# Re-ordered instructions and loads of batches 0 and 1, and a last quarter block split in three, in a linear-attention and gated-MLP kernel

## Chip, cores, metric

One core of a Trainium2 chip. The metric is device time in microseconds of one execution, median of several. A program on one core gives single runs that agree within about 0.35%.

## The reference

```python
q_s = exp(q - max(q, -1)); q_s /= sum(q_s, -1)          # batch 8, heads 8, seq 576, dim 64
k_s = exp(k - max(k,  2)); k_s /= sum(k_s,  2)
kv  = einsum('bhsd,bhse->bhde', k_s, v)
x   = einsum('bhsd,bhde->bhse', q_s, kv)                # to (4608, 512)
h   = x @ w_in                                          # 512 -> 2048
g   = h * sigmoid(beta * h)
out = g @ w_out                                         # 2048 -> 512
```

## The kernel before

Rows are worked in nine chunks: 512 positions of each batch, and the 64-row tails of all eight together. For each chunk TensorE makes x (4 tiles), then h in 16 slices j, each from 4 matmuls over kt; ScalarE makes the tanh, VectorE g, and TensorE adds g times w_out into accumulators ("acc"). The first two batches have their own code, written out instruction by instruction: each engine runs its own list in the order in which it is written. Heads go in pairs: `tpe` transposes the normalised q of a pair, `kvz_mm` makes its kv in 64x64 tiles of the array, `xpe` its x. Banks of PSUM are named by hand.

```python
def kvz_mm(b, j, tag=None, n=1):            # n pairs share one PSUM tile
    ...
    for i in range(RW):                     # 9
        for e in range(2):                  # the two heads: two 64x64 tiles of the array
            r = slice(e * D, (e + 1) * D)
            nc.tensor.matmul(t[r, 0, :], ek[b][r, j, ds(i * D, D)], va[b][r, j, i, :], ...,
                             tile_position=(e * D, e * D))

def kvz_norm(b, j, n=1):                    # VectorE: reciprocal, two multiplies into kvp
    ...
def warm(n, tag):                           # dummy 128x512 matmuls
    ...
# --- cut: the front, batch 0 (excerpt around h of w_in block 1) ---
    hpe(0, 4, [0], "b3")                    # j 4, kt 0, PSUM bank b3
    ...
    hpe(0, 5, [0], "b1")
    hpe(0, 5, [1])
    w_castk(1, 2, A)                        # ScalarE casts w_in block 1, kt 2
    ...
    hpe(0, 7, [0], "b2")
    ...
    hpe(0, 7, [1])
    hpe(0, 4, [2])                          # the first that needs that cast
    ...
    mm_b(0, 0)                              # the first acc matmuls
# --- cut: the end, last chunk; the fourth row block of 128 is two halves of 256 columns ---
    for st in range(1, R + 1):
        for j in range(HOLD + (st == 1), NJ):   # HOLD = 8: earlier j were done in the loop
            mm_b(LASTC, j, [st])
        store(LASTC, st)
```

The softmax here doesn't subtract the row's maximum and nothing guards it: scores larger than these inputs give would overflow.

## Time and profile before

| | before |
|---|---|
| median of the first 3 runs | 282.67 us (281.89 to 282.89) |
| span of the profiled run | 280.6 us |
| TensorE busy | 275.9 us, 98% |
| VectorE, ScalarE, GpSimd busy | 62%, 58%, 14% |
| first acc matmul of chunk 0 / of chunk 1 | 22.23 us / 50.22 us |
| start of the last copy, to the end of the span | 277.49, 3.11 us |

The kernel is a stream of TensorE matmuls with hardly a hole, so the useful marks are the starts of certain matmuls in the TensorE timeline: the first transposes (the dummies are over), the first acc of chunk 0 (the front is over), the first acc of chunk 1 (batch 1 is prepared), the last copy. Their differences tell where time goes to within about 0.05 us, which run times do not: these scatter by 1 us.

### The profile page before, as it was taken

How to read it: one execution, taken by the hardware profiler on the slowest of the kernel's cores; microseconds unless marked ns; L12 is line 12 of the kernel's file. 1: busy time of each engine (PE TensorE's matmuls, PEld its weight loads, DVE VectorE, ACT ScalarE, POOL GpSimd, SP SyncE). 2: the span in 40 equal slices, each digit the busy share in tenths (PEclk: the TensorE clock that was granted, in tenths of full speed). 3: DMA queues.
4: the chain of work that ended last, by engine and by line, in shares of the span. 5: the costliest groups of instructions: out<-in, count | busy, mean ns of one | idle time of the engine just before them, and what ended most of it. 6: DMA issues, size and time to landing. Idle time of an engine off the chain costs nothing.

```text
span 280.6 us, 4450 instructions
## 1 busy us (share of the span) xinstructions
PE 275.9 (98%) x1728; PEld 128.6 (46%) x1728; DVE 175.1 (62%) x284; ACT 162.8 (58%) x248; POOL 38.7 (14%) x58
## 2 busy tenths in 40 slices
PE   8999999999999999999999999999999999999995
PEld 2544454444444444444444444444444544445543
DVE  3864796994478446945595549553864596354361
ACT  4667985958486447744684559444733574454451
POOL 1554236133030003000300030000000000000000
PEclk9999999999999999999999999999999999999999
DMA  7999999999981993199418951641154034005003
GB/s 249 390 394 391 387 388 311 321 292 213 269 240 46 238 287 90 75 233 265 141 78 191 280 167 75 132 94 79 71 89 139 1 151 75 0 0 152 0 0 150
DMA packets 55172, 50.09 MB, mean 179 GB/s; under 512 B 26600, under 2 KB 47344, under 8 KB 55152
## 3 DMA queue, kind: packets, MB, share of 16 engines
q1 hardware_dynamic: 54224, 48.91, 59.8%
q10 hardware_dynamic: 928, 0.92, 0.9%
q8 instruction: 13, 0.21, 0.3%
q14 instruction: 7, 0.06, 0.1%
HBM read 36.71 MB, written 9.44 MB: 164 GB/s over the span
## 4 chain that ended last, share of the span: by engine, by line
PE 98%; DVE 1%; ACT 0%; issue 0%
PE h L403 44%; PE acc L452 43%; PE warm L531 3%; PE kv L341 2%; PE x L372 1%; PE acc L444 1%; PE kv L316 1%; PE x L388 1%; PE tp L297 1%; DVE eq L267 0%; DVE qsT L173 0%; ACT o L171 0%; DVE xT L612 0%; PE x L363 0%; PE tb L564 0%
## 5 line engine op out<-in xcount | busy, mean ns | idle before, releaser
L417 DVE SCALAR_TENSOR_TENSOR g<-th,h 128x512 bf16<-128x512 bf16 x144 | 96.2, 681 | 80.1 <-ACT th L413 79.8
L413 ACT ACTIVATE th<-h,beta_t 128x512 bf16<-128x512 f32 x144 | 97.9, 687 | 81.9 <-PE h L403 81.0
L403 PE MATMUL h<-xT,w_in_b 128*128 128x512 bf16 x576 | 143.2, 379 | 0.0
L452 PE MATMUL acc<-w_out_b,g 128*128 128x512 bf16 x560 | 141.0, 379 | 0.0
L403 PEld LDWEIGHTS <-w_in_b 128*128 128x128 bf16 x576 | 56.3, 98 | 66.4 <-ACT w_in_b L171 0.6
L452 PEld LDWEIGHTS <-g 128*128 128x128 bf16 x560 | 53.8, 98 | 66.0 <-issue 2.5
L173 POOL CAST va<-v_st 128x2048 bf16<-128x2048 f32 (+2 forms) x14 | 17.4, 1257 | 115.2 <-DMA v_st<-in_v_dram 115.2
L261 DVE TENSOR_REDUCE rq<-eq 128x16 f32<-128x1024 bf16 (+1 forms) x20 | 22.1, 1104 | 5.6 <-ACT eq L250 5.1
L267 DVE TENSOR_TENSOR eq<-eq,rq 128x1024 bf16<-128x1024 bf16 (+1 forms) x20 | 23.1, 1157 | 0.1
L171 ACT CAST xT<-x 128x512 bf16<-128x512 f32 x18 | 9.9, 588 | 17.8 <-PE x L372 14.9
L250 ACT ACTIVATE eq<-q_st 128x1024 bf16<-128x1024 f32 (+1 forms) x18 | 16.9, 955 | 2.9 <-DMA q_st<-in_q_dram 2.9
L173 DVE COPY o<-acc 128x512 f32<-128x512 f32 (+1 forms) x19 | 12.3, 660 | 3.6 <-PE acc L452 3.4
L171 ACT COPY o<-acc 128x512 f32<-128x512 f32 (+1 forms) x18 | 9.6, 577 | 8.4 <-PE acc L452 5.0
L173 DVE CAST xT<-x 128x512 bf16<-128x512 f32 x18 | 11.5, 684 | 2.5 <-PE x L372 1.8
L192 ACT ACTIVATE ek<-k_st 128x1024 bf16<-128x1024 f32 x12 | 12.6, 1051 | 0.0
L531 PE MATMUL warm<-xT 128*128 128x512 bf16 x30 | 10.0, 493 | 1.2 <-DVE xT L612 1.2
L173 POOL CAST w_in_b<-w_in 128x512 bf16<-128x512 f32 (+1 forms) x9 | 5.9, 663 | 4.9 <-DMA w_in<-in_moe_w_in_dram 4.7
L531 PEld LDWEIGHTS <-xT 128*128 128x128 bf16 x30 | 3.5, 122 | 6.1 <-issue 3.8
L173 POOL CAST w_out_b<-w_out 128x1024 bf16<-128x1024 f32 x5 | 5.2, 1041 | 7.4 <-DMA w_out<-in_moe_w_out_dram 7.4
L262 DVE RECIPROCAL rq<-rq 128x16 f32<-128x16 f32 (+1 forms) x20 | 4.9, 243 | 0.7
L341 PEld LDWEIGHTS <-ek 128*64 128x64 bf16 x192 | 4.1, 111 | 2.5 <-issue 2.5
L185 ACT ACTIVATE ek<-k_st 128x576 bf16<-128x576 f32 x8 | 5.1, 677 | 0.2 <-DMA k_st<-in_k_dram 0.2
(48 smaller groups left out, 83.1 us busy)
## 6 DMA issues: line engine op xcount, KB each, us to landing
out_dram<-o SPq DMA_DIRECT2D x14, 512.0 KB, 3.4
q_st<-in_q_dram SPq DMA_DIRECT2D x25, 256.0 KB, 4.2
k_st<-in_k_dram SPq DMA_DIRECT2D x6, 1024.0 KB, 9.2
v_st<-in_v_dram SPq DMA_DIRECT2D x6, 1024.0 KB, 11.3
w_in<-in_moe_w_in_dram SPq DMA_DIRECT2D x6, 512.0 KB, 9.6
v_st<-in_v_dram SPq DMA_DIRECT2D x8, 288.0 KB, 8.3
w_out<-in_moe_w_out_dram SPq DMA_DIRECT2D x4, 512.0 KB, 9.0
w_out<-in_moe_w_out_dram SPq DMA_DIRECT2D x2, 1024.0 KB, 9.3
```

Of the source, the lines that this page charges most:

```text
L171: eng.copy(dst, src)
L173: eng.tensor_copy(dst, src)
L192: nc.scalar.activation(ek[b][:, :, h, :].rearrange("p i h d -> p h i d"), k_st[b][:, h, 0 : R * D].rearrange("p h (i d) -> p h i d", i=R), ...
L250: nc.scalar.activation(eq[b][:, :, s * m : (s + 1) * m, :].rearrange("p i h d -> p h i d"), q_st[b][:, s * m : (s + 1) * m, :].rearrange(" ...
L261: nc.vector.tensor_reduce(rq[b][:, 0, :, h], eq[b][:, :, h, :], axis=AX.X, op=ALU.add)
L267: eng.tensor_tensor(eq[b][:, :, h, :], eq[b][:, :, h, :], rq[b][:, 1, :, h].unsqueeze(3).to_broadcast((P, R, m, D)), ALU.mult,)
L341: nc.tensor.matmul(t[r * D : (r + 1) * D, j, :], ek[b][:, i, hd, :] if i < R else ekt[(b // 2) % 2][:, ds(hd * D, D)], va[b][:, i, hd, :] ...
L403: nc.tensor.matmul(h[:], w_unit(j, kt), x_of(c)[:, kt, :], start=(kt == 0), stop=(kt == KT - 1),)
L413: nc.scalar.activation(th[:], h_of[c, j][:], ACTF.Tanh, scale=beta_t[:, j : j + 1])
L417: nc.vector.scalar_tensor_tensor(out=g[:], in0=th_of.pop((c, j))[:], scalar=1.0, in1=h_of[c, j][:], op0=ALU.add, op1=ALU.mult)
L452: nc.tensor.matmul(acc[st][:], g[:, ds(st * P, P)], w_out_b[:, j, :], start=(j == 0), stop=(j == NJ - 1),)
L531: nc.tensor.matmul(t[:], xT[2][:, 0, 0:P], xT[2][:, 0, :])
```

## The change

Its intent: give each engine an order fitted to landings of loads measured before, visit the 64x64 mode less often (batch 0: pairs 0 and 1 together; batch 1: pairs 0, 1, 2 in one run), and end with a shorter last piece. One dummy matmul less. The loads of batch 1 and w_out are re-ordered to match. Core of the diff:

```diff
+    ENDS = ((0, DM // 2), (DM // 2, DM // 4), (3 * DM // 4, DM // 4))
...
-    HB, AB = ["b1", "b2"], ["b0", "b3"]
+    HB, AB = ["b2", "b1"], ["b0", "b3"]
...                                        # store of the last chunk
+                last = st == R - 2 + len(ENDS)
+                evac(nc.scalar if last else nc.vector, o[:, R - 1, cols], acc[st][:, 0:hw])
...                                        # loads: beta before v of pair 1; k of batch 1 ahead of w_out
+    load_kv(k_st, k, 1, "k_st", [0])
     w_load("out", 1)
+    w_load("out", 2)
     load_q(1, 2, [0])
...                                        # front
-    warm(10, tag="acc2")
+    warm(8, tag="acc2")
...
+    warm(2, tag="acc0")
+    kvz_mm(0, 0, "acc3", 2)
     kz_exp(0, 2)
+    kvz_mm(0, 1)
...
+    hpe(0, 4, [0], "acc0")
...
     hpe(0, 5, [0], "b1")
     hpe(0, 5, [1])
...
+    th_act(0, 1)
+    hpe(0, 5, [2])                        # j 7 comes only later
...                                        # batch 1
+    kvz_mm(1, 0, "b0", 2)
+    kvz_mm(1, 1)
+    kvz_mm(1, 2, "b1", 1)
...
+    kvz_norm(1, 0, 2)
+    tpe(1, 3, "b2")
+    tpe(1, 2, "b3")
...
+    q_ev(1, 3, V)
+    xpe(1, 0, "b0")
+    q_ev(1, 2, V)
+    xpe(1, 1, "b2")
...
+    kvz_mm(1, 3, "b3", 1)
...                                        # the end
-    for st in range(1, R + 1):
-        for j in range(HOLD + (st == 1), NJ):
+    for st in range(1, R + 2):
+        if st > R:                         # the last 128 columns: all 16 j at the end
+            acc_of[LASTC].append(ps.tile([P, DM], F32, tag=bank("h"), ...))
+        for j in range(HOLD + (st == 1) if st <= R else 0, NJ):
             mm_b(LASTC, j, [st])
         store(LASTC, st)
```

More of the change, by code (lines that the diff above doesn't have):

```diff
@@ L442, in mm_b @@
             if c == LASTC and st >= R - 1:
-                hw = DM // 2
+                lo, hw = ENDS[st - R + 1]
                 nc.tensor.matmul(
@@ L446, in mm_b @@
                     g[:, ds((R - 1) * P, P)],
-                    w_out_b[:, j, ds((st - R + 1) * hw, hw)],
+                    w_out_b[:, j, ds(lo, hw)],
                     start=(j == 0),
@@ L507, in store @@
             if st >= R - 1:
-                hw = DM // 2
-                k_ = st - R + 1
-                cols = ds(k_ * hw, hw)
-                evac((nc.vector, nc.scalar)[k_], o[:, R - 1, cols], acc[st][:, 0:hw])
-                (nc.sync, nc.scalar)[k_].dma_start(ov[:, R - 1, cols], o[:, R - 1, cols])
+                lo, hw = ENDS[st - R + 1]
+                cols = ds(lo, hw)
+                last = st == R - 2 + len(ENDS)
+                evac(nc.scalar if last else nc.vector, o[:, R - 1, cols], acc[st][:, 0:hw])
+                (nc.scalar if last else nc.sync).dma_start(ov[:, R - 1, cols], o[:, R - 1, cols])
                 return
@@ L577 @@
     load_kv(v_st, v, 0, "v_st", [0])
+    nc.sync.dma_start(beta_r[:], moe_beta.rearrange("(hh q) -> hh q", q=2 * P))
     load_kv(v_st, v, 0, "v_st", [1])
     load_kv(v_st, v, 0, "v_st", [2])
-    nc.sync.dma_start(beta_r[:], moe_beta.rearrange("(hh q) -> hh q", q=2 * P))
     load_kv(v_st, v, 0, "v_st", [3])
@@ L589 @@
     w_load("out", 0, 1)
+    w_load("in", 2, 1)
     w_load("in", 2, 0)
-    w_load("in", 2, 1)
+    w_load("in", 3, 0)
     w_load("in", 3, 1)
-    w_load("in", 3, 0)
+    load_kv(k_st, k, 1, "k_st", [0])
     w_load("out", 1)
+    w_load("out", 2)
     load_q(1, 2, [0])
-    w_load("out", 2)
+    load_kv(k_st, k, 1, "k_st", [1])
     load_q(1, 2, [1])
+    w_load("out", 3, 0)
+    load_kv(k_st, k, 1, "k_st", [2])
+    load_kv(v_st, v, 1, "v_st", [1])
+    load_kv(v_st, v, 1, "v_st", [0])
     load_kv(v_st, v, 1, "v_st", [2])
-    w_load("out", 3, 0)
-    load_kv(k_st, k, 1, "k_st", [0])
-    load_kv(v_st, v, 1, "v_st", [0])
-    load_kv(k_st, k, 1, "k_st", [2])
-    load_kv(k_st, k, 1, "k_st", [1])
-    load_kv(v_st, v, 1, "v_st", [1])
-    w_load("out", 3, 1)
     load_kv(k_st, k, 1, "k_st", [3])
     load_kv(v_st, v, 1, "v_st", [3])
+    w_load("out", 3, 1)
     load_q(2)
@@ L621 @@
     q_sum(0, 0, 4)
-    q_exp(0, 3, 4)
     q_mul(0, 0, 4)
     q_exp(0, 2, 4)
-    q_sum(0, 3, 4)
-    tpe(0, 0, "acc3")
     q_exp(0, 1, 4)
     q_sum(0, 2, 4)
+    tpe(0, 0, "acc3")
+    q_exp(0, 3, 4)
+    q_sum(0, 1, 4)
     q_ev(0, 0, A)
-    q_sum(0, 1, 4)
     q_mul(0, 2, 4)
+    q_mul(0, 1, 4)
+    warm(8, tag="acc2")
+    tpe(0, 2, "acc3")
     kz_exp(0, 0)
-    q_mul(0, 1, 4)
-    warm(10, tag="acc2")
-    tpe(0, 2, "acc3")
-    kz_exp(0, 1)
     q_ev(0, 2, V)
-    vz_cast(0, 0, G)
     warm(1, tag="acc1")
@@ L640 @@
     tpe(0, 1, "acc2")
+    kz_exp(0, 1)
+    vz_cast(0, 0, G, part=0)
+    q_sum(0, 3, 4)
+    beta_pe("acc1")
+    vz_cast(0, 0, A, part=1)
+    vz_cast(0, 1, G, part=0)
+    vz_cast(0, 1, A, part=1)
     q_mul(0, 3, 4)
+    warm(2, tag="acc0")
+    kvz_mm(0, 0, "acc3", 2)
     kz_exp(0, 2)
-    warm(1, tag="acc1")
-    kvz_mm(0, 0, "acc3", 1)
-    vz_cast(0, 1, G)
-    q_ev(0, 1, V)
-    tpe(0, 3, "acc1")
-    kz_exp(0, 3)
-    kvz_norm(0, 0)
-    kvz_mm(0, 1, "acc2", 1)
-    vz_cast(0, 2, G)
@@ L652 @@
-    q_ev(0, 3, A)
-    beta_pe("acc0")
-    kvz_norm(0, 1)
-    kvz_mm(0, 2, "acc3", 1)
-    vz_cast(0, 3, A, part=1)
-    vz_cast(0, 3, G, part=0)
-    beta_ev()
-    xpe(0, 0, "acc1")
+    kvz_mm(0, 1)
+    vz_cast(0, 2, G, part=0)
+    tpe(0, 3, "acc0")
+    vz_cast(0, 2, A, part=1)
+    kvz_norm(0, 0, 2)
+    q_ev(0, 1, A)
+    kvz_mm(0, 2, "b3", 1)
+    vz_cast(0, 3, G)
+    kz_exp(0, 3)
+    xpe(0, 0, "b2")
     kvz_norm(0, 2)
-    kvz_mm(0, 3, "acc2", 1)
+    xpe(0, 1, "acc3")
     w_castk(0, 0, G)
@@ L663 @@
     xev(0, 0, A)
-    xpe(0, 1, "acc0")
-    kvz_norm(0, 3)
-    xpe(0, 2, "b3")
-    xev(0, 1, A)
-    hpe(0, 0, [0], "b0")
-    hpe(0, 1, [0], "b1")
-    xev(0, 2, V)
-    w_castk(0, 1, A)
+    kvz_mm(0, 3, "acc2", 1)
+    xev(0, 1, V)
+    q_ev(0, 3, A)
+    xpe(0, 2, "b3")
+    w_castk(0, 1, G)
+    hpe(0, 1, [0], "b0")
+    kvz_norm(0, 3)
+    hpe(0, 0, [0], "b1")
+    beta_ev()
+    xev(0, 2, A)
+    hpe(0, 3, [0], "b2")
+    hpe(0, 1, [1])
+    w_castk(0, 2, A)
     xpe(0, 3, "acc3")
-    w_castk(0, 2, G)
@@ L674 @@
-    hpe(0, 3, [0], "b2")
+    hpe(0, 3, [1])
+    w_castk(0, 3, G)
     xev(0, 3, V)
-    hpe(0, 2, [0], "acc0")
     hpe(0, 0, [1])
-    w_castk(0, 3, G)
-    hpe(0, 3, [1])
+    hpe(0, 2, [0], "b3")
     hpe(0, 3, [2])
-    hpe(0, 1, [1])
-    hpe(0, 1, [2])
-    hpe(0, 1, [3])
-    hpe(0, 3, [3])
-    th_act(0, 1)
-    w_castk(1, 0, G)
+    hpe(0, 2, [1])
     hpe(0, 0, [2])
     hpe(0, 0, [3])
-    hpe(0, 2, [1])
-    w_castk(1, 1, G)
-    th_act(0, 3)
-    hpe(0, 2, [2])
-    g_dve(0, 1)
-    hpe(0, 2, [3])
@@ L695 @@
-    hpe(0, 4, [0], "b3")
-    th_act(0, 0)
+    w_castk(1, 0, G)
+    hpe(0, 2, [2])
+    th_act(0, 0)
+    hpe(0, 2, [3])
+    hpe(0, 3, [3])
+    w_castk(1, 1, G)
+    hpe(0, 4, [0], "acc0")
+    th_act(0, 2)
+    hpe(0, 1, [2])
+    g_dve(0, 0)
+    hpe(0, 1, [3])
+    w_castk(1, 3, G)
     hpe(0, 4, [1])
-    g_dve(0, 3)
-    w_castk(1, 3, G)
+    w_castk(1, 2, A)
+    g_dve(0, 2)
     hpe(0, 5, [0], "b1")
     hpe(0, 5, [1])
-    w_castk(1, 2, A)
-    g_dve(0, 0)
-    hpe(0, 7, [0], "b2")
@@ L705 @@
-    th_act(0, 2)
-    hpe(0, 7, [1])
-    hpe(0, 4, [2])
-    hpe(0, 5, [2])
-    hpe(0, 4, [3])
-    g_dve(0, 2)
-    hpe(0, 5, [3])
-    th_act(0, 4)
+    th_act(0, 1)
+    hpe(0, 5, [2])
+    hpe(0, 4, [2])
+    th_act(0, 3)
+    hpe(0, 4, [3])
+    g_dve(0, 1)
+    hpe(0, 5, [3])
+    hpe(0, 7, [0], "b3")
+    th_act(0, 4)
+    hpe(0, 7, [1])
+    g_dve(0, 3)
     hpe(0, 7, [2])
+    w_cast("out", 0, 0, G)
     hpe(0, 7, [3])
+    th_act(0, 5)
+    g_dve(0, 4)
     hpe(0, 6, [0], "b0")
-    w_cast("out", 0, 0, G)
@@ L717 @@
-    th_act(0, 5)
     hpe(0, 6, [1])
-    g_dve(0, 4)
+    th_act(0, 7)
     hpe(0, 6, [2])
+    g_dve(0, 5)
     hpe(0, 6, [3])
-    th_act(0, 7)
-    g_dve(0, 5)
     mm_b(0, 0)
-    th_act(0, 6)
-    w_cast("out", 0, 1, G)
+    w_cast("out", 0, 1, A)
     g_dve(0, 7)
     mm_b(0, 1)
+    th_act(0, 6)
+    w_castk(2, 2, A)
+    mm_b(0, 2)
     g_dve(0, 6)
+    w_castk(2, 3, A)
+    mm_b(0, 3)
     w_castk(2, 0, A)
     w_castk(2, 1, G)
-    mm_b(0, 2)
-    mm_b(0, 3)
-    w_castk(2, 2, A)
-    w_castk(2, 3, G)
@@ L736 @@
-    hpe(0, 11, [0, 1, 2, 3], "b0")
-    w_cast("in", 3, 1, A)
-    hpe(0, 10, [0, 1, 2, 3], "b1")
+    hpe(0, 8, [0, 1, 2, 3], "b0")
+    w_cast("in", 3, 0, A)
+    hpe(0, 10, [0, 1, 2, 3], "b1")
+    th_act(0, 8)
+    hpe(0, 11, [0, 1, 2, 3], "b2")
+    w_cast("in", 3, 1, G)
+    th_act(0, 10)
+    g_dve(0, 8)
+    hpe(0, 9, [0, 1, 2, 3], "b3")
     th_act(0, 11)
-    hpe(0, 8, [0, 1, 2, 3], "b2")
-    w_cast("in", 3, 0, G)
-    th_act(0, 10)
+    g_dve(0, 10)
+    kz_exp(1, 0)
+    hpe(0, 12, [0, 1, 2, 3], "b0")
@@ L743 @@
     g_dve(0, 11)
-    hpe(0, 9, [0, 1, 2, 3], "b3")
-    th_act(0, 8)
-    g_dve(0, 10)
-    hpe(0, 13, [0, 1, 2, 3], "b0")
-    g_dve(0, 8)
     th_act(0, 9)
-    hpe(0, 14, [0, 1, 2, 3], "b1")
+    hpe(0, 13, [0, 1, 2, 3], "b1")
+    th_act(0, 12)
     g_dve(0, 9)
+    hpe(0, 15, [0, 1, 2, 3], "b2")
+    g_dve(0, 12)
+    w_cast("out", 1, 1, A)
+    w_cast("out", 1, 0, G)
+    hpe(0, 14, [0, 1, 2, 3], "b0")
+    th_act(0, 15)
     th_act(0, 13)
-    w_cast("out", 1, 0, G)
-    w_cast("out", 1, 1, A)
@@ L755 @@
-    hpe(0, 15, [0, 1, 2, 3], "b2")
+    mm_b(0, 4)
+    g_dve(0, 15)
+    th_act(0, 14)
+    mm_b(0, 5)
     g_dve(0, 13)
-    mm_b(0, 4)
-    th_act(0, 14)
-    th_act(0, 15)
+    w_cast("out", 2, 1, G)
+    w_cast("out", 2, 0, A)
+    mm_b(0, 6)
     g_dve(0, 14)
-    mm_b(0, 5)
     q_exp(1, 0)
-    g_dve(0, 15)
-    mm_b(0, 6)
+    mm_b(0, 7)
+    mm_b(0, 8)
+    kz_exp(1, 1)
     q_sum(1, 0)
-    mm_b(0, 7)
-    w_cast("out", 2, 1, A)
-    w_cast("out", 2, 0, G)
-    hpe(0, 12, [0, 1, 2, 3], "b0")
+    mm_b(0, 9)
@@ L770 @@
+    q_exp(1, 1)
     q_mul(1, 0)
-    q_exp(1, 1)
-    mm_b(0, 8)
-    vz_cast(1, 2, G, part=0)
-    vz_cast(1, 2, A, part=1)
-    mm_b(0, 9)
-    q_sum(1, 1)
-    th_act(0, 12)
-    tpe(1, 0, "b1")
-    w_cast("out", 3, 0, A)
-    tpe(1, 1, "b2")
-    mm_b(0, 10)
-    q_ev(1, 0, V)
-    q_mul(1, 1)
-    kz_exp(1, 0)
-    mm_b(0, 11)
-    vz_cast(1, 0, G, part=0)
-    vz_cast(1, 0, A, part=1)
-    q_ev(1, 1, A)
-    g_dve(0, 12)
-    kvz_mm(1, 0, "b1", 1)
-    kz_exp(1, 2)
-    tpe(1, 3, "b3")
@@ L793 @@
-    kvz_norm(1, 0)
-    tpe(1, 2, "b2")
-    mm_b(0, 12)
-    kz_exp(1, 1)
-    q_ev(1, 3, V)
-    q_ev(1, 2, V)
-    kvz_mm(1, 2, "b0", 1)
-    vz_cast(1, 1, A, part=1)
-    vz_cast(1, 1, G, part=0)
-    xpe(1, 0, "b1")
-    kvz_norm(1, 2)
-    kvz_mm(1, 1, "b2", 1)
-    xev(1, 0, A)
-    mm_b(0, 13)
-    kvz_norm(1, 1)
-    w_cast("out", 3, 1, G)
-    hpe(1, 0, [0], "b0")
-    xpe(1, 2, "b1")
+    mm_b(0, 10)
+    mm_b(0, 11)
+    w_cast("out", 3, 0, G)
+    q_sum(1, 1)
+    kz_exp(1, 2)
+    tpe(1, 0, "b0")
@@ L811 @@
+    tpe(1, 1, "b1")
+    mm_b(0, 12)
+    q_ev(1, 0, A)
+    vz_cast(1, 1, G, part=0)
+    q_ev(1, 1, V)
+    vz_cast(1, 1, A, part=1)
+    q_mul(1, 1)
+    mm_b(0, 13)
+    vz_cast(1, 0, G)
+    vz_cast(1, 2, A, part=1)
+    vz_cast(1, 2, G, part=0)
+    kvz_mm(1, 0, "b0", 2)
+    kvz_mm(1, 1)
+    kvz_mm(1, 2, "b1", 1)
     kz_exp(1, 3)
-    xpe(1, 1, "b2")
-    xev(1, 2, V)
-    mm_b(0, 14)
+    kvz_norm(1, 0, 2)
+    tpe(1, 3, "b2")
+    tpe(1, 2, "b3")
     vz_cast(1, 3, A, part=1)
     vz_cast(1, 3, G, part=0)
-    xev(1, 1, V)
@@ L818 @@
-    kvz_mm(1, 3, "b1", 1)
+    q_ev(1, 3, V)
+    xpe(1, 0, "b0")
+    q_ev(1, 2, V)
+    xpe(1, 1, "b2")
+    xev(1, 0, A)
+    kvz_norm(1, 2)
+    kvz_mm(1, 3, "b3", 1)
+    xev(1, 1, A)
+    hpe(1, 0, [0], "b0")
+    w_cast("out", 3, 1, G)
+    kvz_norm(1, 3)
+    xpe(1, 2, "b1")
+    hpe(1, 0, [1])
+    hpe(1, 3, [0], "b2")
+    xev(1, 2, V)
+    xpe(1, 3, "b3")
+    mm_b(0, 14)
+    xev(1, 3, V)
     mm_b(0, 15)
-    kvz_norm(1, 3)
-    hpe(1, 2, [0], "b2")
+    hpe(1, 0, [2])
     store(0, 0)
-    xpe(1, 3, "b1")
+    hpe(1, 0, [3])
@@ L824 @@
+    hpe(1, 2, [0], "b1")
+    hpe(1, 2, [1])
+    th_act(1, 0)
+    store(0, 1)
     hpe(1, 1, [0], "b3")
     hpe(1, 1, [1])
-    xev(1, 3, A)
-    store(0, 1)
     hpe(1, 1, [2])
-    hpe(1, 0, [1])
-    hpe(1, 0, [2])
-    hpe(1, 0, [3])
+    g_dve(1, 0)
+    hpe(1, 1, [3])
     store(0, 2)
-    hpe(1, 1, [3])
-    hpe(1, 3, [0], "b1")
-    th_act(1, 0)
-    store(0, 3)
     hpe(1, 3, [1])
     hpe(1, 3, [2])
+    th_act(1, 1)
+    store(0, 3)
     hpe(1, 3, [3])
-    th_act(1, 1)
-    g_dve(1, 0)
@@ L842 @@
-    hpe(1, 2, [1])
     hpe(1, 2, [2])
+    hpe(1, 2, [3])
     th_act(1, 3)
-    hpe(1, 2, [3])
     g_dve(1, 1)
@@ L955 @@
     store(LASTC, 0)
-    for st in range(1, R + 1):
-        for j in range(HOLD + (st == 1), NJ):
+    for st in range(1, R + 2):
+        if st > R:
+            acc_of[LASTC].append(ps.tile([P, DM], F32, tag=bank("h"), bufs=1, name=f"acc{LASTC}_{st}"))
+        for j in range(HOLD + (st == 1) if st <= R else 0, NJ):
             mm_b(LASTC, j, [st])
```

## The prediction

> **What bounds the kernel now.** I read the page first (busy shares, slices, chain), then the totals of waits, then the timeline of TensorE alone over the first 50 us and over the last 10.
>
> ```profile
> PE 275.9 (98%) x1728; PEld 128.6 (46%) x1728; DVE 175.1 (62%) x284; ACT 162.8 (58%) x248; POOL 38.7 (14%) x58
> PE   8999999999999999999999999999999999999995
> PEclk9999999999999999999999999999999999999999
> PE 98%; DVE 1%; ACT 0%; issue 0%
> ```
>
> TensorE is full in 38 of 40 slices at full clock, and the chain that ended last is 98% TensorE. No other engine is over 62%. So only three things can move the time: TensorE work that goes away, stretches in which its queue waits, and what comes after its last matmul. A busy row does not show the second, because a 128x512 matmul is recorded as 379 ns although its successor starts earlier: 28 matmuls in the chain take 6.04 us, 0.216 us each. I therefore read starts, not durations. From the TensorE timeline (start, length, operation, in brackets the idle time before it):
>
> ```profile
> 7.92 0.39 PE L297 MATMUL tp<-identity,eq 128*128 128x128 bf16 x4
> 8.14 2.32 PE L531 MATMUL warm<-xT 128*128 128x512 bf16 x10
> ...
> 11.29 0.48 PE L316 MATMUL kv<-va,ek 64*64 64x65 bf16 x18
> 12.14 0.40 PE L297 MATMUL tp<-identity,eq 128*128 128x128 bf16 x4 [0.37 <-DVE eq L267]
> ...
> 15.52 6.88 PE L403 MATMUL h<-xT,w_in_b 128*128 128x512 bf16 x30
> 22.23 3.62 PE L452 MATMUL acc<-w_out_b,g 128*128 128x512 bf16 x16
> ...
> 40.91 1.03 PE L452 MATMUL acc<-w_out_b,g 128*128 128x512 bf16 x4
> 41.86 0.47 PE L316 MATMUL kv<-va,ek 64*64 64x65 bf16 x18
> 42.27 0.39 PE L388 MATMUL x<-qsT,kvp 128*128 128x512 bf16 x1
> ```
>
> Three rates come from it. Eight transposes take 0.45 us (40.45 to 40.91 in the same view), 0.056 each. The 40-matmul kv groups of later batches take 0.76 us, so a small kv matmul costs 0.019 to 0.020 and 18 of them 0.36. Four acc matmuls from 40.91 end their slots at 41.77, yet kv starts at 41.86: 0.09 to enter the 64x64 mode. kv start to next start is 0.41, so 0.05 to leave it. One visit to that mode thus costs about 0.15 us beyond its matmuls.
>
> Stretch 7.92 to 22.23 (14.31 us): 16 transposes 0.89, 12 warm 2.59, 72 kv 1.44, two beta transposes 0.32 (12.97 to 13.29), 36 x and h matmuls 7.77; sum 13.01. The other 1.30 is four mode visits (0.60), the wait at 12.14 (11.70 to 12.14, 0.44) and 0.24 within the 30 h matmuls (6.71 against 6.47). Stretch 25.69 to 47.20 (21.51 us): 86 large matmuls 18.55, 16 transposes 0.90, 72 kv 1.44; the remaining 0.6 is again four mode visits. There is no other wait in it. From there on slots are back to back, until the tail:
>
> ```profile
> 275.54 1.91 PE L444 MATMUL acc<-w_out_b,g 128*128 128x256 bf16 x16
> 277.07 0.33 SPq L512 DMA_DIRECT2D out_dram<-o  x1
> 277.49 0.37 ACT L171 COPY o<-acc 128x256 f32<-128x256 f32 x1 [2.89 <-PE acc L444]
> 277.89 0.36 ACTq L512 DMA_DIRECT2D out_dram<-o  x1
> ```
>
> The last matmul slot ends about 277.3. One copy, one store and the landing make up the last 3.1 of 280.6 us.
>
> **What the Trainium skill says.** "TensorE: Matmul & The Clock Gate", section "Wait — 56ns, not 53.3ns?", gives start-to-start spacing when warm of 55.6 ns at N = 128 and 215.7 ns at N = 512: the trace agrees (0.056, 0.216). "TensorEngine Tiling (Array Packing)", section "Key Properties", says "Changing tiling mode (not just tile) drains the TensorE"; it gives no figure, and the trace shows the 0.15 us per visit. "DMA: Bandwidth & Descriptors", section "Anatomy of one DMA — SWDGE (gpsimd) path", splits a transfer into about 2.0 us fixed and bytes / 436e9, fitted for transfers issued from GpSimd; the last stores here, issued from SyncE and ScalarE, land in 1.8 to 2.5 us, which is near it. "GPSIMD Engine Reference", section "Specifications", has GpSimd share its SBUF interfaces with VectorE, with contention when VectorE has two SBUF inputs; here a 128x320 cast on POOL takes 0.46 us alone and 1.42 at 35.63, while the two-input multiply of q (35.52, 1.23 us) runs.
>
> **The change, part by part.**
>
> (a) *Front, fewer dummies and visits.* Warm matmuls after the first 18 go from 10+1+1 to 8+1+2: -1 x 0.216 = -0.22. Pairs 0 and 1 of batch 0 share one visit: four become three, -0.15.
>
> (b) *Front, waits.* I walked the new order by hand with the durations above and the same landings (v pairs about 0.75 us apart from 9.85, w_in of block 0 from 12.7 every 0.66). TensorE reaches the transposes of pair 3 at about 12.15, but the sum of pair 3 now follows the copy of pair 2 on VectorE (10.3 to 10.7), then sum 0.69, reciprocal 0.2, multiply 0.7 to 1.0: about 12.4. Wait 0.3, in place of 0.44. The normalisation of pair 3 now stands behind an x copy (0.65): about 0.2 before x of pair 3. ScalarE casts w_in 1 of kt 2 after two tanh, near 19.4, while TensorE wants it near 19.1: 0.25. Sum 0.75 against 0.68 before. The author's order was drawn up from measured landings, and my walk errs by 0.2 at each step; I take 0.5, so -0.2.
>
> (c) *Batch 1, visits.* Pairs 0, 1, 2 in one visit: four become two, -0.30.
>
> (d) *Batch 1, waits.* Before has none. In the new order h14 takes the PSUM bank of h12 two j later instead of having the whole acc stretch between. From the start of an h to the end of its g takes 2.47 us (25.69 to 28.16) and two h in between allow 2.59; but the k exponential of pair 0 (0.68) sits before tanh 9, which delays tanh 12 by some 0.4: a wait of 0 to 0.3. After the run of three, x of pair 1 takes the bank of the transposes of pair 3, whose copy (0.42) stands on VectorE behind the joint normalisation (about 0.65): 0.2, and 0.1 more before kv of pair 3. I take 0.3 for all of (d).
>
> (e) *Loads.* When a cast waited for its load tells when the load landed:
>
> ```profile
> 29.33 1.04 POOL L173 CAST w_out_b<-w_out 128x1024 bf16<-128x1024 f32 x1 [1.61 <-DMA w_out<-in_moe_w_out_dram]
> 33.39 1.04 POOL L173 CAST w_out_b<-w_out 128x1024 bf16<-128x1024 f32 x1 [3.02 <-DMA w_out<-in_moe_w_out_dram]
> 43.47 0.46 POOL L173 CAST va<-v_st 128x320 bf16<-128x320 f32 x1 [0.51 <-DMA v_st<-in_v_dram]
> ```
>
> So blocks 1 and 2 of w_out landed near 29.3 and 33.4, the last v pair near 43.4. The bytes ahead of the first load of batch 2 are the same, so the last landing stays near 43.4. w_out block 1 lands 0.75 later (30.1, a 288 KB pair of k at the 390 GB/s of these slices being put ahead of it), but its first use moves from 31.7 to about 32.5, since h12 now goes first. w_out block 2 lands about 0.6 sooner, used at 36. The second half of block 3 now lands last, near 43.4, and is cast by 44.5; its use is near 45.4. Nothing is added, but margins are about 1 us.
>
> (f) *End.* Columns are unchanged: 32 x 256 become 16 x 256 and 32 x 128. A 256 slot is 0.11 (1.76 us for 16), a 128 slot 0.056: +0.03 in all. The last copy shrinks from 256 to 128 columns: 512 take 0.59 and 256 take 0.37, so about 0.26, -0.11. The last store halves to 64 KB: by the DMA page's bytes / 436e9 an estimate of -0.15, of which I count 0.1. The other quarter's store starts 16 x 0.056 = 0.9 us sooner and lies beside this. Sum -0.18.
>
> Sum: -0.22 - 0.15 - 0.2 - 0.30 + 0.3 + 0.03 - 0.11 - 0.1 = -0.75 with waits as taken; with waits as walked (0.75, 0.6) it is about -0.2. I weigh the two equally: -0.5.
>
> **The rivals.** *A wait takes the place of each one removed.* For it: all engines run in order, POOL and VectorE contend over v casts and the q multiply (now near 40 us, just before the run of three), and three pairs must be ready together. Time then 282.3 to 283. *A late landing holds TensorE*, such as v of pair 2 or beta (now wanted near 10.5 instead of 12.97, and issued about 1.2 us sooner): each such miss adds 0.3 to 1 us. For it: DMA is saturated at 390 GB/s up to 22 us. Against it: the load order was changed for just this. *The new order has no waits left*: -0.9 in the front, -0.3, -0.2: 281.1. In all of them the 225 us in the middle stay as they are, so none comes near 2%, which would be 5.7 us.
>
> **Range and chances.** The three runs and the profiled one average 282.45 (spread 1.0). Less 0.5 that is 282.0. Waits are uncertain by 0.5, the median of few runs by 0.3: 281.3 to 282.8. Faster by 2% would need more than all the waits there are (1% chance); slower by 2% a missed landing of over 5 us (1%).
>
> **What would show it.** Right: the TensorE timeline has the first acc group at about 21.9 (22.23 before), 11 warm matmuls after the first transposes, three kv visits in batch 0 and two in batch 1, and the first acc of chunk 1 at 49.5 to 50.1 (50.22 before); from there to the last 128x512 matmul the same length as before; the final copy about 0.26. Wrong: idle time at kv or h12 to h14 ahead of 50 us of more than 0.8 in sum, a wait of TensorE put down to a DMA, a visit that costs much less than 0.15, or a last store that lands no sooner.

## The result, and the profile after

The changed kernel took 282.19 us (median of 4, 282.10 to 282.81), the kernel before 282.50 (median of 4 in all). The ratio of the fast runs is 0.9996 with a 95% interval of 0.9972 to 1.002: the same. (A ratio is the mean time of one kernel's fast runs over the mean of the other's of the same rounds, so not quite the ratio of the medians.) The span of the profiled run went from 280.6 to 280.3. Line numbers in the new kernel are one higher from the diff's first line on.

The page after, its busy shares and the row of TensorE in 40 slices:

```profile
PE 275.7 (98%) x1743; PEld 128.6 (46%) x1743; DVE 174.6 (62%) x278; ACT 163.6 (58%) x251; POOL 37.3 (13%) x57
PE   8999999999999999999999999999999999999995
```

Nothing changed at this height: 15 matmuls more (16 from the split end, one dummy less), the same full row. The TensorE timeline after, over the front and batch 1 (start, length, operation, idle before it):

```profile
8.02 0.39 PE L298 MATMUL tp<-identity,eq 128*128 128x128 bf16 x4
8.24 1.89 PE L532 MATMUL warm<-xT 128*128 128x512 bf16 x8
...
11.59 0.77 PE L317 MATMUL kv<-va,ek 64*64 64x65 bf16 x36
12.72 0.40 PE L298 MATMUL tp<-identity,eq 128*128 128x128 bf16 x4 [0.36 <-DVE eq L268]
...
22.05 3.62 PE L453 MATMUL acc<-w_out_b,g 128*128 128x512 bf16 x16
...
41.59 1.24 PE L317 MATMUL kv<-va,ek 64*64 64x65 bf16 x54
42.76 0.62 PE L298 MATMUL tp<-identity,eq 128*128 128x128 bf16 x8
43.25 0.83 PE L389 MATMUL x<-qsT,kvp 128*128 128x512 bf16 x2
44.12 0.48 PE L317 MATMUL kv<-va,ek 64*64 64x65 bf16 x18
```

The merged visits are there (36 and 54 kv matmuls in a row, 18 in every visit before) and waits are, too: 0.36 at 12.72; the pair of x at 43.25 lasts 0.83 where such a pair lasts 0.60, so the second x starts 0.23 late; and kv starts at 44.12, about 0.11 after the slot and the mode switch allow. The tail after, all engines:

```profile
275.05 2.38 PE L445 MATMUL acc<-w_out_b,g 128*128 128x256 bf16 x32
277.46 0.27 ACT L172 COPY o<-acc 128x128 f32<-128x128 f32 x1 [3.35 <-PE acc L445]
277.76 0.36 ACTq L513 DMA_DIRECT2D out_dram<-o  x1
```

| mark (us) | before | after | difference |
|---|---|---|---|
| first transposes | 7.92 | 8.02 | +0.10 |
| first acc of chunk 0 | 22.23 | 22.05 | -0.18 |
| from there to first acc of chunk 1 | 27.99 | 28.11 | +0.12 |
| from there to the last copy | 227.27 | 227.30 | +0.03 |
| last copy to end of span | 3.11 | 2.84 | -0.27 |
| span | 280.6 | 280.3 | -0.3 |

So in this one pair of traces the front and the end gain and batch 1 loses. My first theory was this table read as it stands: the front won its 0.2 to 0.3 us by a dummy, a visit and a wait less; batch 1 saved 0.30 in visits and paid 0.43 in new waits, one of them for a PSUM bank; the end won by its shorter last copy and store. The rivals: loads that land late hold the front or batch 1 whatever the order; and the 0.15 us per visit, which was read off as a remainder, is not what a visit costs.

### The profile page after: what moved, and what is told of

Read it like the earlier page. It is cut to its first block, busy times and chain, and to the rows that moved or that the text cites. A ratio compares the mean times of both kernels' runs of the same rounds, so it can differ in the third digit from the quotient of the medians.

```text
span 280.3 us, 4471 instructions
## 1 busy us (share of the span) xinstructions
PE 275.7 (98%) x1743; PEld 128.6 (46%) x1743; DVE 174.6 (62%) x278; ACT 163.6 (58%) x251; POOL 37.3 (13%) x57
## 4 chain that ended last, share of the span: by engine, by line
PE 97%; DVE 2%; ACT 0%; issue 0%; ACTq 0%
PE h L404 44%; PE acc L453 43%; PE warm L532 3%; PE kv L342 2%; PE x L373 1%; PE acc L445 1%; PE kv L317 1%; PE x L389 1%; PE tp L298 0%; DVE eq L268 0%; DVE qsT L174 0%; DVE g L418 0%; ACT th L414 0%; DVE rq L262 0%; DVE kvp L332 0%
## 5 line engine op out<-in xcount | busy, mean ns | idle before, releaser
L174 POOL CAST va<-v_st 128x320 bf16<-128x320 f32 (+2 forms) x14 | 16.5, 1181 | 112.3 <-DMA v_st<-in_v_dram 112.2
L174 DVE COPY o<-acc 128x512 f32<-128x512 f32 (+2 forms) x20 | 12.7, 642 | 4.2 <-PE acc L453 4.0
L174 POOL CAST w_in_b<-w_in 128x512 bf16<-128x512 f32 (+1 forms) x8 | 5.3, 666 | 7.6 <-DMA w_in<-in_moe_w_in_dram 7.5
```

The source lines that it names most:

```text
L174: eng.tensor_copy(dst, src)
```

## The experiments

Twelve kernels ran, all with correct results, in four calls; each call's kernels shared a chip and the runs of the kernel before. Edits are against the kernel named.

| run | base and edit | median us | before, same call | ratio (95%) |
|---|---|---|---|---|
| e1_end | before + new end | 281.90 | 282.03 | 0.9990 (0.9975 to 1.0005) |
| e2_front | before + new front | 282.24 | 282.03 | 1.0000 (0.9982 to 1.0018) |
| e3_batch1 | before + new batch 1 | 282.51 | 282.03 | 1.0011 (0.9992 to 1.0029) |
| e4_visits | before + ten visits | 284.42 | 282.03 | 1.0080 (1.0065 to 1.0095) |
| e5_bank | after, banks swapped | 282.82 | 282.04 | 1.0027 (1.0010 to 1.0044) |
| e6_nowarm2 | after, two dummies less | 282.87 | 282.04 | 1.0027 (1.0012 to 1.0042) |
| e7_sum3 | the same, a sum earlier | 282.70 | 282.04 | 1.0022 (1.0007 to 1.0037) |
| e8_front_end | before + new front and end | 282.26 | 282.04 | 1.0012 (0.9996 to 1.0028) |
| e9_two_early | e8, two h matmuls earlier | 282.11 | 282.10 | 0.9993 (0.9979 to 1.0006) |
| e10_end5 | e1 again | 282.35 | 282.10 | 1.0001 (0.9987 to 1.0014) |
| e11_after5 | after again | 282.57 | 282.10 | 1.0014 (1.0001 to 1.0026) |
| e12_bank_h4 | e9, another bank for h 4 | 282.39 | 282.05 | 1.0008 (0.9994 to 1.0021) |

The marks from each kernel's one trace ("cast" is the start of ScalarE's cast of w_in block 1, kt 2, explained below; "end" runs from the last copy to the end of the span):

| kernel | first transposes | cast | first acc | acc minus cast | to chunk 1 | end |
|---|---|---|---|---|---|---|
| before | 7.92 | 19.31 | 22.23 | 2.92 | 27.99 | 3.11 |
| e1_end | 7.71 | 18.93 | 21.85 | 2.92 | 28.06 | 2.88 |
| e3_batch1 | 7.75 | 19.21 | 22.13 | 2.92 | 28.11 | 3.09 |
| e4_visits | 7.12 | 19.06 | 21.90 | 2.84 | 28.06 | 3.12 |
| e10_end5 | 7.32 | 18.93 | 21.85 | 2.92 | 28.07 | 2.87 |
| after | 8.02 | 18.73 | 22.05 | 3.32 | 28.11 | 2.84 |
| e2_front | 6.75 | 18.80 | 22.07 | 3.27 | 28.06 | 3.11 |
| e5_bank | 7.98 | 18.81 | 22.09 | 3.28 | 28.82 | 2.88 |
| e6_nowarm2 | 7.54 | 19.05 | 22.32 | 3.27 | 28.10 | 2.87 |
| e7_sum3 | 6.95 | 18.86 | 22.14 | 3.28 | 28.10 | 2.85 |
| e8_front_end | 6.94 | 18.90 | 22.17 | 3.27 | 28.06 | 2.86 |
| e9_two_early | 7.67 | 18.87 | 22.05 | 3.18 | 28.08 | 2.86 |
| e11_after5 | 7.75 | 19.38 | 22.66 | 3.28 | 28.10 | 2.83 |
| e12_bank_h4 | 7.32 | 18.73 | 21.57 | 2.84 | 28.42 | 2.90 |

### The parts one by one

**e1_end**: only the `ENDS` parts of the diff.

> The kernel before with the new end alone (last 128 columns accumulated whole at the end). Theory: TensorE work is unchanged, so the last copy starts within 0.05 us of 277.49 as counted from the same first acc matmul; the copy takes 0.27 instead of 0.37; in all 0.1 to 0.3 us less span. Rival A (the last store's fixed time is what counts, and the tail hides nothing): the store lands no sooner although the copy is shorter, below 0.1. Rival B (32 small matmuls with their own weight loads cost more than 0.056 each): last copy starts 0.2 us or more later.

**e2_front**: only the loads and orders of batch 0 up to the casts of w_in block 2.

> The kernel before with the new front alone (orders of batch 0 and its loads up to the first acc matmuls, beta moved up). Theory: counted from the first transpose of q to the first acc matmul 14.03 us as in the changed kernel (14.31 before), so the first acc at 22.0 to 22.1, and everything behind moves by the same 0.2 to 0.3 us, the first acc of chunk 1 at about 49.95. Rival: batch 1 waits for loads, so the lead is lost by then and that group starts at 50.2 again.

**e3_batch1**: only the loads from w_in block 3 on, the order from h 8 on, and the two swapped banks.

> The kernel before with the new load order and instruction order of batch 1 alone. Theory: two visits to the 64x64 mode less (-0.30) and new waits of TensorE near the x matmuls (+0.43), so the first acc of chunk 1 at about 50.35 (50.22 before), 0.1 us more in all. Rival: the waits in the changed kernel come from the front being early; with the old front they are not there, and that group starts at about 49.9.

Measured. The end is as the theory has it: over all traces, the last copy is followed by 3.09 to 3.12 us with the old end and 2.83 to 2.90 with the new, 0.25 less. 0.10 of this is the copy (0.37 to 0.27); the rest, about 0.15, is put down to the store of half the size. The run time agrees (0.13 us less), but its interval includes none.

The new front alone did not do what was expected: no gain in run time, and the first acc at 22.07 although the first transposes came at 6.75, 1.3 us sooner than in the changed kernel's first trace. (From chunk 1 to the last copy this trace took 227.46, 0.15 to 0.19 more than the others. That is one wait: the acc matmul at 59.38 starts 0.18 late, after a g that VectorE finished at 59.32; VectorE was late because its q multiply at 56.09 took 2.63 us instead of 1.21 beside a GpSimd cast of v begun at 55.73; more on this pair under e5_bank.) The gain that the first pair of traces showed was not a property of the order. That refuted the first half of my theory, and I looked for what holds the front.

Batch 1 alone loses 0.05 us against the old batch 1 in traces other than that of before (28.11 against 28.06), with the old front: so its waits do not come from an early front. The direction was right; I had expected first acc of chunk 1 at 50.35 and it was 50.24, because the front of that trace was 0.1 us sooner.

### What a visit to the narrow mode costs

**e4_visits**: in the kernel before, the kv groups of five later stages are cut.

```diff
+            if between is not None and j < HP - 1:
+                between(j)                       # after pairs 0 and 1 of the kv group
...
-                kv_mm(n + 2, f"acc{R - 1}")
+                kv_mm(n + 2, f"acc{R - 1}", lambda st: mm_b(c, 14, [st]) if st < R - 2 else None)
...
-                mm_b(c, j)
+                mm_b(c, j, [R - 2] if j == 14 else None)
```

> The kernel before with the kv group of each of five later stages cut in three by two acc matmuls that came a few places later before: the same matmuls, ten more visits to the narrow mode, no dependency near. Theory: 0.10 to 0.15 us for each visit, 1.0 to 1.5 us in all, and kv to acc starts in the trace that show it. Rival: what looked like a switch cost was a wait for data, or the cost is hidden when a group is short; under 0.4 us in all.

Measured: +0.8%, 2.25 us between chunk 1 and the last copy (229.52 against 227.27): 0.225 us for each of ten visits, more than both expectations. The TensorE timeline of this run at one cut:

```profile
99.84 0.32 PE L341 MATMUL kv<-va,ek 128*64 128x65 bf16 x8
99.99 0.20 PE L341 MATMUL kv<-vt,ekt 128*64 128x65 bf16 x2
100.12 0.39 PE L454 MATMUL acc<-w_out_b,g 128*128 128x512 bf16 x1
100.44 0.32 PE L341 MATMUL kv<-va,ek 128*64 128x65 bf16 x8
```

Ten kv matmuls in an uncut group take 0.155 us from start to start. Here the acc follows after 0.28, so leaving the mode costs 0.125, and the next kv starts 0.32 after the acc, whose slot is 0.216, so entering costs about 0.105. The same can be read for the 64x64 mode of batches 0 and 1: a lone visit of 18 takes 0.41 from its start to the next matmul's, and the run of 54 in e5_bank takes 0.99. So a matmul takes (0.99 - 0.41) / 36 = 0.016, not 0.020, and leaving costs 0.41 - 18 x 0.016 = 0.12. With about 0.095 to enter, a visit costs 0.21, where the prediction had 0.15. (The prediction got 0.019 to 0.020 from 0.76 us for 40 matmuls, start to next start, which includes leaving that mode.) Batch 1 thus saves 0.42 by its two visits less, and what it pays must be larger, too.

### What batch 1 pays

**e5_bank**: in the changed kernel.

```diff
-    xpe(1, 1, "b2")          # bank of the transposes of pair 3
+    xpe(1, 1, "b3")          # bank of the transposes of pair 2, copied out second
-    kvz_mm(1, 3, "b3", 1)
+    kvz_mm(1, 3, "b2", 1)
...                           # h(1,3), x(1,3), h(1,1) follow suit
```

> The changed kernel with two PSUM banks of batch 1 swapped: x of pair 1 takes the bank of the transposes of pair 2, which are copied out second, and kv of pair 3 takes the bank of pair 3's. Theory (the wait of 0.23 us before x of pair 1 is for the bank, and the bank is freed by the copy): x of pair 1 starts at about 44.0 instead of 43.7, and the first acc of chunk 1 about 0.2 us later than 50.16. Rival (the wait is for the joint normalisation of kv, or for an instruction queue): x of pair 1 stays at 43.7 and nothing moves.

Its timeline, TensorE and GpSimd:

```profile
40.36 2.69 POOL L174 CAST va<-v_st 128x576 bf16<-128x576 f32 x3 [0.30 <-DMA v_st<-in_v_dram]
42.13 1.06 PE L317 MATMUL kv<-va,ek 64*64 64x65 bf16 x54 [0.45 <-POOL va L174]
...
43.79 0.39 PE L389 MATMUL x<-qsT,kvp 128*128 128x512 bf16 x1
44.57 0.38 PE L389 MATMUL x<-qsT,kvp 128*128 128x512 bf16 x1 [0.39 <-DVE qsT L174]
```

The second x now starts 0.78 us after the first, against 0.45 before the swap, and the trace names the copy of the transposes: the wait is for the bank. (That it started at 44.57 and not at 44.0 is due to the first line: the kv run began 0.5 us late in this execution, after its v casts.) That late start was not meant and shows a second cost of the new order. The v casts of pairs 0 and 2 on GpSimd now fall into the time of VectorE's two-input multiply of q: three casts took 2.69 us here, where a 128x320 cast alone takes 0.46. In the eight traces with such a pair in batch 1 that were looked at, the one that starts first keeps its own time and the other waits for it. Here the multiply started at 40.34 (1.22 us) and the 128x576 cast at 40.36, and the cast took 1.72. In the first trace of the changed kernel that cast started first, at 40.24 (0.67 us), and the multiply at 40.31 took 1.68; the next cast, behind the multiply, took 1.30 instead of 0.46 and made the third pair of the kv run 0.17 late (the run took 1.17 instead of 0.99). So less than 0.1 us in the starts decides which engine pays. In the six traces with the new batch 1 TensorE lost 0.5, 0.17 and 0.05 us to it, and nothing in three.

The account of batch 1 from e3_batch1: two visits less -0.42 and 0.08 less of an old wait before kv; 0.22 before the first x (normalisation), 0.23 before the second (bank), 0.11 before kv of pair 3: sum +0.06, measured +0.05.

### What holds the front

**e6_nowarm2**: the changed kernel without `warm(2, tag="acc0")`.

> The changed kernel without the two warm matmuls before the kv matmuls of batch 0 (0.43 us of TensorE). Theory: they fill time in which VectorE prepares pair 3; the wait before the transposes of pair 3 grows from 0.36 to about 0.8 us and the first acc matmul stays within 0.05 us of 14.03 us after the first transpose. Rival (TensorE work counts as such, as the prediction took one warm matmul for 0.22): first acc 0.4 us sooner.

**e7_sum3**: also `q_sum(0, 3, 4)` moved ahead of `q_ev(0, 2, V)`.

> As the run without two warm matmuls, and the sum of pair 3 put before the copy of pair 2 on VectorE, into its idle 0.5 us. Theory: the transposes of pair 3 need not wait any more, the normalisation of kv of pairs 0 and 1 starts when their kv is done, x of pair 0 starts about 0.4 us sooner than before (5.4 us after the first transpose now); of this the first acc matmul keeps 0.1 to 0.4, because the casts of block 1 of w_in wait for a load that lands near 18.6. Rival: the loads hold all of it, first acc unchanged; or the path is not through VectorE and x of pair 0 does not move.

**e8_front_end**: e1_end and e2_front together.

> The new front and the new end with the old batch 1, which is the version that beats both kernels if the theory holds: -0.28 in the front, -0.15 at the end, nothing from batch 1: 0.1 us less than the changed kernel, 0.4 less than the kernel before, first acc of chunk 1 at about 49.95. Rival: as in the run with the front alone, batch 1 loses the lead.

All three missed in detail. As a ruler I had taken the first transposes, and these move from 6.75 to 8.02 us between executions, since the 18 dummies before them start 0.43 us apart at first and 0.216 apart later, and the change comes after the 9th of them in e2_front and after the 15th in the changed kernel's first trace. In e6 the wait before the transposes of pair 3 was gone, not longer; in e7 x of pair 0 started 6.16 us after the first transposes, where I had expected about 5.0. But the first acc was not sooner in any of them (22.32, 22.14, 22.17). In run time e6 and e7 are even slower than the kernel before, by 0.8 and 0.7 us with intervals above 1; the trace is of the fastest of the four runs in both, and where the other runs lost more was not traced. The lines of e8_front_end, all engines, show why:

```profile
18.90 0.62 ACT L172 CAST w_in_b<-w_in 128x512 bf16<-128x512 f32 x1 [1.03 <-DMA w_in<-in_moe_w_in_dram]
18.93 0.61 POOL L174 CAST w_in_b<-w_in 128x512 bf16<-128x512 f32 x1 [1.64 <-DMA w_in<-in_moe_w_in_dram]
...
19.57 2.76 PE L404 MATMUL h<-xT,w_in_b 128*128 128x512 bf16 x12 [0.92 <-ACT w_in_b L172]
...
22.17 0.59 PE L453 MATMUL acc<-w_out_b,g 128*128 128x512 bf16 x2
```

Both engines that cast the second half of w_in block 1 idle for the load, and start when it lands. TensorE idles for the cast and has twelve h matmuls left, 12 x 0.216 = 2.6 us. In the new front, as the diff has it, the first acc is the start of ScalarE's cast plus 3.27 us in every trace, within 0.05, whatever came before. That start is the landing in all these traces but one, the changed kernel's first:

```profile
18.65 0.61 POOL L174 CAST w_in_b<-w_in 128x512 bf16<-128x512 f32 x1 [0.50 <-DMA w_in<-in_moe_w_in_dram]
18.73 0.62 ACT L172 CAST w_in_b<-w_in 128x512 bf16<-128x512 f32 x1
```

There the load had landed by 18.65, and the cast came 0.08 later, right behind two tanhs: with less work in front of it the first acc could have gained 0.08 us at most. The changed kernel run again (e11_after5) is the clearest case:

> The changed kernel once more, in five rounds on the same chip: within 0.3 us of the kernel before, first acc 3.3 us after the start of the cast of w_in block 1, kt 2, and the first acc of chunk 1 28.1 us after that.

```profile
19.38 0.62 ACT L172 CAST w_in_b<-w_in 128x512 bf16<-128x512 f32 x1 [1.10 <-DMA w_in<-in_moe_w_in_dram]
...
20.06 2.77 PE L404 MATMUL h<-xT,w_in_b 128*128 128x512 bf16 x12 [0.99 <-ACT w_in_b L172]
22.66 3.62 PE L453 MATMUL acc<-w_out_b,g 128*128 128x512 bf16 x16
```

The same kernel, a cast that starts 0.65 us later than in its first trace because the load landed later, the first acc 0.61 later, the span 280.9 instead of 280.3. Both marks came as expected (3.28 and 28.10), the time a little worse than the 0.3 us I allowed. The old order leaves only ten matmuls behind that cast (2.84 to 2.92), since j 7 goes ahead of it. In the trace of before the load was not even what held it: GpSimd had cast its part at 17.76 without waiting for a load, while ScalarE was busy with tanhs:

```profile
17.59 1.84 ACT L413 ACTIVATE th<-h,beta_t 128x512 bf16<-128x512 f32 x3 [1.63 <-PE h L403]
17.76 0.62 POOL L173 CAST w_in_b<-w_in 128x512 bf16<-128x512 f32 x1
...
19.31 0.62 ACT L171 CAST w_in_b<-w_in 128x512 bf16<-128x512 f32 x1
```

In e1_end, e3_batch1 and e10_end5, too, the cast starts right behind the third tanh; of the five traces with the old front only e4_visits has ScalarE waiting there, 0.14 us. So the load can be in by 17.8 or as late as 19.4, and the old front, which reaches that point later, minds it less. Two things stay open. With the old front the load was in before 17.8 in two of five traces, with the new one never before 18.65 in nine; whether the new order of loads delays it was not tested. And no run took a dummy or a visit alone out of the old front, where in four of five traces the load did not hold this cast.

**e9_two_early** and **e12_bank_h4** test that account on the new front with the old batch 1 and the new end:

```diff
+    hpe(0, 7, [0], "b3")
+    hpe(0, 7, [1])
     hpe(0, 5, [2])
...
-    hpe(0, 7, [0], "b3")
-    hpe(0, 7, [1])
```

> The new front and end with the old batch 1, and two h matmuls of w_in block 1, kt 0 and 1 (their casts are done by 18.2), moved ahead of the first one that needs the cast of kt 2. Theory: the front is held by the load of the second half of w_in block 1, whose cast starts at 18.7 to 19.3 in all ten traces; the first acc follows that cast by its 0.65 us and the h matmuls that the order leaves behind it, ten in the old order (2.84 to 2.92 us measured from the cast's start) and twelve in the new (3.27 to 3.32). With ten left behind again it follows by about 2.85, near 21.75, so 0.4 us sooner than the same kernel without the move, of which up to 0.2 may be lost to the casts of block 2. Rival: the front is held by TensorE's own work or by VectorE, and the order of these two changes nothing. If the early start meets g of pair 2 (the bank is its), the gain is smaller in executions where the clock ramps late.

Measured: the first acc followed the cast by 3.18, not 2.85. The h matmuls were over earlier, but another wait took the place. TensorE timeline of e9_two_early:

```profile
22.05 3.63 PE L453 MATMUL acc<-w_out_b,g 128*128 128x512 bf16 x16 [0.17 <-DVE g L418]
```

The diff puts h of j 4 into the bank of the first accumulator; that bank comes free with g of j 4, and its tanh stands on ScalarE behind the cast that waits for the load. e12 gives j 4 the bank of the fourth accumulator:

```diff
-    hpe(0, 4, [0], "acc0")
+    hpe(0, 4, [0], "acc3")
```

> The run with two matmuls moved ahead, and h of j 4 in the PSUM bank of the fourth accumulator instead of the first. There the first acc waited for g of j 4 (done at about 22.0), because both use one bank; g comes late since ScalarE runs the tanhs behind the cast that waits for the load. Theory: with another bank the first acc no longer waits for that g and follows the start of the cast of w_in block 1, kt 2 by about 2.85 us (3.18 there), the fourth accumulator's first matmul comes three slots later and waits 0 to 0.1; first acc of chunk 1 0.2 to 0.3 us sooner relative to the cast, span about 280.0. Rival: the first acc is held by the cast of w_out or by the other g, and nothing moves; or the casts of w_in block 2 take the gain back before chunk 1.

```profile
19.41 2.33 PE L404 MATMUL h<-xT,w_in_b 128*128 128x512 bf16 x10 [0.17 <-ACT w_in_b L172]
21.57 3.62 PE L453 MATMUL acc<-w_out_b,g 128*128 128x512 bf16 x16
25.37 0.82 PE L404 MATMUL h<-xT,w_in_b 128*128 128x512 bf16 x3 [0.18 <-ACT w_in_b L172]
```

Now the first acc follows the cast by 2.84, as expected: 21.57 is the earliest of all. Then most of it is lost at the next cast: the h matmuls of w_in block 2 wait for it until 25.37, about where they start with the old front (25.31 in e1_end and e10_end5). From first acc to chunk 1 it takes 28.42 instead of 28.06. This second wait is not for a load. That cast, of kt 0, starts at 24.67, although kt 1 of the same load is cast by GpSimd from 24.08 on: ScalarE has worked without a hole since the landing at 18.73 (a cast, five tanhs, a cast of w_out, a tanh, two casts), while GpSimd idled 2.98 us before 24.08. The new front gives ScalarE four of the six casts of w_out block 0 and w_in block 2, the old one two. The rival named in the expectation, that block 2 takes the gain back, is what happened to most of it, and the run time (1.0008) shows none.

**e10_end5** repeats the end alone in five rounds.

> The kernel before with the new end alone once more, in five rounds: 0.2 us less than the kernel before (last copy 0.10 and last store 0.15 less, last copy starting 0.03 later); it should be no slower than the changed kernel, since the new front leaves two more matmuls behind the load (+0.4 against +0 there, less what the old front loses to waits) and the new batch 1 is 0.05 longer.

Measured: 1.0001 (0.9987 to 1.0014), its trace at a span of 280.1. The 0.2 us of the end stand in every trace, but the run times do not resolve them. No kernel here was faster than the kernel before clear of noise (e4 to e7 and e11 were slower, clear of it, though by less than 2%); the traces with the lowest spans are those of the end alone (280.1, twice), and whether it is the best version stays open.

## Why the prediction was right or wrong

The range and the verdict were right (282.19 measured, 282.0 predicted), but that says little: the range, 281.3 to 282.8, also holds the 282.50 of the kernel before. That the sum came near is luck, since the front did not give its part. Of the marks, the first acc (22.05) came near the predicted 21.9; the first acc of chunk 1, at 50.16, lies outside 49.5 to 50.1. By its steps:

- *What bounds the kernel*: right for the middle 225 us, which did not move (227.27 to 227.31 from chunk 1 to the last copy in all traces with unchanged visits but e2_front, with its one wait for a g). Incomplete for the front: a TensorE row without holes was read as "TensorE work that goes away" making time, but before 22 us the work in it can be a dummy or an early real matmul ahead of a load.
- *(a) front, -0.37 for a dummy and a visit*: the step that failed. Both went away, but in the new front neither is on the path. The first acc comes 3.27 us after the cast of w_in block 1, kt 2, which waits for its load in every trace but one, and there comes 0.08 us after the landing; taking two more dummies away (e6) did not bring the first acc nearer to the cast (3.27). The rival "a late landing holds TensorE" was the right one, though I looked for it at v and beta. Beta is not shown to hold anything: the 0.10 us before its transposes at 10.72 is there in eight of nine traces with the new front, wherever between 10.02 and 10.72 they start, so it does not follow a landing; entering the 64x64 mode takes the same 0.095.
- *(b) front waits, walked as 0.75*: the first trace has 0.76 (0.10 before the beta transposes, 0.36, 0.09, 0.21), near enough. The agreement is partly luck, since other executions divide the time otherwise. I discounted it to 0.5 for no reason but the author's skill, which made the forecast of the front too good.
- *(c) visits in batch 1, -0.30*: mis-sized; a visit costs 0.21 us, so -0.42. The error is in the pace of the small matmuls, taken as 0.020 from another mode with its leaving counted in, and measured as 0.016.
- *(d) batch 1 waits, walked as 0.6 and taken as 0.3*: 0.54 to 0.56 in traces. The bank of pair 3's transposes (0.23 against 0.2 walked) and kv of pair 3 (0.11 against 0.1) were as walked. Nothing happened at h 14, where I had walked up to 0.3 (its 32 h matmuls take 6.91 us, all slots full). The normalisation, or the v casts against the q multiply, cost 0.2 instead.
- *(e) loads of batch 1*: right in the main: the last landing came at 43.83, where 43.4 was predicted; w_out never held TensorE.
- *(f) the end, -0.18*: right in kind, 0.25 at the end less 0.03 in slots. The copy gave 0.10 of the 0.11 predicted; the store gave the whole 0.15 of the page's bytes term, of which I had counted 0.1. That it is the size of the store and not something else behind the copy was not tested apart.
- *The middle way between waits as walked (-0.2) and waits as taken (-0.75)*: the walk was right. By stage the change is worth nothing, or a loss, in the front (first acc at 22.05 to 22.66 in five traces of it, mean 22.2; 21.85 to 22.23 in five of the old one, mean 22.0), +0.05 in batch 1, -0.22 at the end; run times give -0.1 us (0.9996) in the first comparison and +0.4 us (1.0014) in the second.

## What to carry to other kernels

Where an engine's row is full because dummies and early work fill it, taking work off it may shorten nothing, as here, because a load behind it lands too late. Find the first cast that idles for a load, and count what the order leaves behind it: two matmuls moved ahead of that point brought the first acc 0.43 us nearer to it (3.27 to 2.84), once their bank was free. Then look at the lists of the other engines behind it: ScalarE's took 0.36 of it back. Merging groups to save a mode switch also merges their results and their banks; here the saving (0.42 us) came back as waits (0.5 us). When one pair of traces shows a gain smaller than the scatter of landings, take marks relative to the landing from several traces before believing it.

## What the Trainium skill lacked or had wrong

- "TensorEngine Tiling (Array Packing)", section "Key Properties", says that a mode switch drains TensorE and gives no figure. Here entering and leaving costs 0.225 us per visit for 128x64 (0.105 and 0.125 at one cut) and about 0.21 for 64x64 (0.095 and 0.12).
- "TensorE: Matmul & The Clock Gate", section "Wait — 56ns, not 53.3ns?", says that start-to-start spacing never drops below about 25 ns however small N is. That does not hold across tiles: with two 64x64 tiles in turn, N = 65, the matmuls came 16 ns apart on average here, in pairs (2 to 8 ns within a pair). For one tile the spacing was 33 ns, which agrees with it; the sentence lacks that distinction. The page's 55.6 and 215.7 ns agree with this case.
- The same page, section "What's actually happening", calls the warm-up variable from run to run. That agrees: the same 18 dummies let the first transposes start at 6.75 to 8.02 us. Nothing is lacking there; it did not matter for the first acc (22.07, 22.17 and 22.05 with first transposes at 6.75, 6.94 and 8.02).
- "DMA: Bandwidth & Descriptors", section "Anatomy of one DMA — SWDGE (gpsimd) path": its bytes / 436e9 gives an estimate of 0.15 us for 64 KB less, and the end of the span moved by about 0.15 with it, on a store issued from ScalarE, so nothing is wrong there. No page says how much the landing of a load deep in a queue varies: the second half of w_in block 1 came at 17.8 us or sooner in a trace of the kernel before and at 19.4 in one of the changed kernel.
